# Accumulating transfers for running outputs, and weights' maxima that cross partitions through DRAM

## The chip, the core and the metric

One core of one Trainium2 chip runs the whole program. The metric is device microseconds of one execution. The core's engines work side by side and each takes its own instructions strictly in order: TensorE (PE in the rows), VectorE (DVE), ScalarE (ACT), GpSimd (POOL) and SyncE (SP), which issues the transfers. Semaphores tie them together.

## The reference

Chunked attention (batch 4, 8 heads, 768 positions of 64, chunks of 32 with 16 positions of left and 8 of right context and 8 memory rows) makes x, 3072 tokens of 512 columns. Then a mixture of eight experts with a Sinkhorn routing P follows, and it is nearly all of the work:

```python
for e in range(E):                      # 8 experts
    h = np.maximum(x @ w1[e], 0.0)      # 3072 x 512 @ 512 x 1024
    ye = h @ w2[e]                      # 3072 x 1024 @ 1024 x 512
    out += P[:, e:e + 1] * ye
```

## The kernel before

**Units.** The expert part runs 48 units: for each of 8 experts 6 groups of 512 tokens, in alternate direction from expert to expert, so that the last group of one expert is the first of the next. A unit has 36.4 to 36.7 us in the kernel's own timetable (`begin`). It makes the hidden layer in four parts fp (`hidden`: banks px, py, pz; reads q and r on ScalarE, sums c on VectorE) and then the outputs of two token tiles at a time (`output`: banks yx, yy, yz; reads y on ScalarE). Every matrix is split into two 16-bit halves (three passes), and products of 2x2 blocks are formed with seven instead of eight multiplications, which is why there are sums of weights (ws, wsi), of hidden blocks (ss) and of products (c, acc). `inner` does the same once more inside one product (banks ix, iy, iz, tile m).

**Running outputs.** For each tile T of 128 tokens a row block `akeep[T]` of 128x512 f32 lies in DRAM. `fetch_acc` loads it into an `acc` tile (ring of four), 12 us ahead of the unit's outputs. `collect` lets GpSimd add the read product q into acc (line 2382) and VectorE then add the bank times the routing factor f (line 2392); the fourth sum of an output is VectorE's alone (line 2426). SP stores acc to `akeep[T]` or, for the last expert, to the output (line 2464). Expert 0 stores without a factor; expert 1 applies it in a ScalarE pass behind the load.

**Weights.** `maxima(e + 1)` is called in the first unit of expert e, is due three units later, and loads the next expert's 4 MB once to find the largest magnitude of each matrix. `scales` turns the per-partition maxima into scales: from expert 1 on GpSimd does `partition_all_reduce` across the partitions, VectorE the rest. Later `load` fetches the weights again, `cut` forms their sums ws on GpSimd (line 747, one ws tile in the ring), and `split` makes the two halves: ScalarE writes the first (line 639), VectorE the second (line 648). `both` adds the sums wsi for the inner products.

**Order.** All instructions are collected as tasks with an engine, a cost in us, a priority and dependencies. `Plan.run` is a list scheduler at build time: it takes at each step the task that can start first, by priority among those that could, and so writes the order of each engine's instructions. `Plan.due` sets priorities back from the time at which TensorE wants a result. Tasks with `port` share an interface of VectorE and GpSimd; the planner lets such a task start only when the other engine's is over, up to 0.3 us. From the unit LATE = 4 on (`turn`, where `plan.fill` is None) attention is over and its memory is given to more buffers. All transfers are issued by SP, in its order.

Of the kernel before, what the change touches and what calls it, by code (L numbers as in the profile page):

```python
# [12 lines left out]
F32 = mybir.dt.float32  # L13
I32 = mybir.dt.int32
AF = mybir.ActivationFunctionType
ALU = mybir.AluOpType
# [24 lines left out]
LAG = 0.04  # L41
FREE = 0.3
SUMS = 0.0
ROUTE = 50
BESIDE = (2,), (3,)
HOLD = 2.0


class Task:
# [61 lines left out]
class Plan:  # L111
# [84 lines left out]
    def due(self):  # L196

        when = {}
        for t in reversed(self.tasks[self.late :]):
            if t.eng == "PE":  # L200
                when[id(t)] = t.prio
                continue
            by = [when[id(s)] for s in t.then if id(s) in when]
            if not by:
                continue
            lag = LANDS + READY + 1.0 if t.dma else LAG + 0.15
            when[id(t)] = min(by) - lag - t.cost
            if t.frees is not None:
                when[id(t)] = min(when[id(t)], t.prio + 200.0 + HOLD)
            if t.eng in ("ACT", "DVE", "POOL"):  # L210
                t.prio = when[id(t)]

    def run(self):
# [10 lines left out]
        while left:  # L224
# [51 lines left out]
            t.start = at  # L276
            if t.size:
                self.count(t.size, at, t.cost)
            if t.port:
                at = max(at, self.held["POOL" if t.eng == "DVE" else "DVE"] - FREE)  # L280
                self.held[t.eng] = at + t.cost
            if t.dma:
                t.start = at = max(at, self.pipe - BEHIND)
# [22 lines left out]
            for s in t.then:  # L306
                s.left -= 1
                late = lag
                if s.eng == t.eng and not t.dma:
                    late = 0.0 if t.eng == "PE" or self.fill is None else LAG  # L310
                elif t.dma and self.fill is not None:

                    late = MARGIN if s.prio - t.end > FAR else RISK if t.end > 10.0 else 0.0
                s.ready = max(s.ready, t.end + late)
                if s.left == 0:
                    for e in s.engines():
                        heappush(waiting[e], (s.ready, s.n, s))
# [4 lines left out]
def tile_chunked_attn_sinkhorn_moe(  # L322
# [135 lines left out]
    def ring(name, slots):  # L458
        rings[name] = Ring(slots)
# [22 lines left out]
    ring("w2", range(4))  # L482
    ring("sm", range(2))
    ring("xi", range(2))
    ring("wi", range(2))

    def buf(kind, pool, shape, dtype, name, slot=None):
# [41 lines left out]
    def scales(part, s, u, name, deps, prio, pool=None, shift=SHIFT):  # L529
# [24 lines left out]
        soon = prio if pool is None else prio - FIRM  # L554
        t = add("DVE", 0.16, most, deps, soon)
        if pool is None:

            def everywhere():
                power(a)
                inverse(a)  # L560

            t = add(
                "POOL",
                14.0,
                lambda: nc.gpsimd.partition_all_reduce(a, m, P, bass_isa.ReduceOp.max),
                [t],
                prio,
                port=False,
            )
            return add("DVE", 1.7, everywhere, [t], prio, port=True)  # L570
# [1716 lines left out]
    def fetch_acc(n, t):  # L2287

        e, u = units[n]
        res = []  # L2290
        for T in (u * TU + t, u * TU + t + TH):
            a = buf("acc", apool, [P, DM], F32, f"acc_{e}_{T}")
            ld = None
            if e > 0:
                ld = add(
                    "SP",
                    1,
                    lambda a=a, T=T: nc.sync.dma_start(a.t, akeep[T]),
                    [akept[T]],
                    outputs_at(n) - 12.0,  # L2300
                    [a],
                    dma=0.95,
                )
            if e == 1:
                ld = add(
                    "ACT",
                    0.73,
                    lambda a=a, T=T: nc.scalar.activation(
                        a.t, a.t, AF.Copy, scale=pscale[:, 0, T : T + 1]
                    ),  # L2310
                    [ld, pscales[0]],
                    outputs_at(n) - 3.0,
                    [a],
                )
            res.append((T, a, ld))
        return res

    def output(n, t, hs):
# [44 lines left out]
            )  # L2363

        lo, hi = slice(0, DH), slice(DH, DM)

        def collect(acc, ld, cols, src, q, deps, f, last=True):

            if e == 0:
# [2 lines left out]
                    0.43,  # L2372
                    lambda: nc.vector.tensor_tensor(acc.t[:, cols], src.t, q.t, op=ALU.add),
                    deps,
                    now[0] - FIRM,
                    [acc, q],
                    frees=src if last else None,
# [41 lines left out]
        c12 = collect(a2, l2, hi, pz, q6, [t3, r6], f2)  # L2419
        yield  # L2420
        t4 = run(px, P4, True, [c22])
        if e > 0:
            c21 = add(
                "DVE",
                0.49,
# [18 lines left out]
        for T, a, deps in ((T2, a2, [c11, c12]), (T1, a1, [c22, c21])):  # L2444
            dst = out[T * P : (T + 1) * P] if e == E - 1 else akeep[T]
            if n == len(units) - 1:

                for cols, dep in zip((lo, hi) if a is a2 else (hi, lo), deps):
# [8 lines left out]
                        [a],  # L2457
                        dma=0.7,
                    )
                continue  # L2460
            akept[T] = add(
                "SP",
# [219 lines left out]
    for n, (e, u) in enumerate(units):  # L2682
# [27 lines left out]
        if n == LATE:  # L2710
# [3 lines left out]
            def turn():  # L2714
                plan.fill = None
                astack.close()
                late["xi"] = ctx.enter_context(tc.tile_pool(name="xr", bufs=1, side="right"))
                late["wi"] = ctx.enter_context(tc.tile_pool(name="wri", bufs=1, side="right"))
                late["w2"] = ctx.enter_context(tc.tile_pool(name="wr2", bufs=1, side="right"))
# [8 lines left out]
            att_tasks = lgs + [xkept[v] for v in range(KEEP)] + list(gkept.values())  # L2728
            opened[0] = add("-", 0.0, turn, att_tasks, -2000.0)
            for kind, slot in (  # L2730
                ("xi", 0), ("xi", 1), ("wi", 0), ("wi", 1), ("w2", 4), ("w2", 5), ("h", 4), ("h", 5), ("c", 2), ("ss", 2)
            ):
                rings[kind].after(slot, [opened[0]])
            for kind in ("c", "ss"):
# [124 lines left out]
```

## Time and profile before

| | |
|---|---|
| time before, three runs | 1918.87 us median (1915.16 to 1921.62) |
| the profiled execution | 1916.56 us, span of its instructions 1914.8 us |
| TensorE's granted clock | 1.000 |
| busy, share of the span | TensorE 98%, VectorE 77%, ScalarE 54%, GpSimd 44% |
| DMA | 262.61 MB, mean 137 GB/s, 215305 packets |
| queues used by transfers | hardware queue 42.8% of the engines' time, instruction fetch under 1% |

A row names the engine, the line, the operation and its tiles as out<-in. A time in brackets is the idle time just before the row, with the instruction that ended it. Matmuls are pipelined and overlap in the rows: one of 256 columns shows 273 ns, while a group of 12 moves on by 1.31 us.

### The profile page before, as it was taken

The page shows a single profiled execution, that of the slowest core. Times are in us where ns is not written, and L with a number is a line of the kernel's source. Part 1 is how long each engine was busy: PE and PEld are TensorE (multiplying, and loading weights), DVE is VectorE, ACT ScalarE, POOL GpSimd, SP SyncE. Part 2 cuts the span into 40 slices and gives each one's busy share as a digit, 9 for nine tenths or more (in the row PEclk, how much of TensorE's full clock was granted, in tenths as well). Part 3 has the DMA queues.
Part 4 walks back from the last instruction along what each step waited for, and adds up shares of the span by engine and source line. Part 5 has one row for each costly group of instructions (what it writes and reads, how often), then busy time and mean ns, then how long its engine had stood idle before and what let it go on. Part 6 is the DMA issues. An engine that isn't in the chain of part 4 may idle for free. (4 is left out here: it accounts for less than half of the span.)

```text
span 1914.8 us, 48313 instructions
## 1 busy us (share of the span) xinstructions
PE 1881.3 (98%) x19931; PEld 1618.2 (85%) x19931; DVE 1476.4 (77%) x2446; ACT 1036.5 (54%) x2077; POOL 843.6 (44%) x851
## 2 busy tenths in 40 slices
PE   8899999999999999999999999999999999999999
PEld 5677667688889989888988989888998889889998
DVE  6887789878789776888579866897668885796565
ACT  6655555654665455555456444654555554564452
POOL 3531222643346444635454453655346354554233
PEclk9999999999999999999999999999999999999999
DMA  9968844244424541363234443245413732322422
GB/s 216 214 138 205 213 143 144 95 143 179 153 67 148 207 148 45 116 231 140 94 107 153 155 141 103 73 167 193 142 46 115 248 123 99 107 95 89 138 84 67
DMA packets 215305, 262.61 MB, mean 137 GB/s; under 512 B 111148, under 2 KB 144940, under 8 KB 210732
## 3 DMA queue, kind: packets, MB, share of 16 engines
q1 hardware_dynamic: 215084, 259.52, 42.8%
q8 instruction: 156, 2.56, 0.6%
q14 instruction: 65, 0.53, 0.1%
HBM read 194.46 MB, written 65.01 MB: 136 GB/s over the span
## 5 line engine op out<-in xcount | busy, mean ns | idle before, releaser
L1900 PEld LDWEIGHTS <-w 128*128 128x128 f16 x7188 | 700.3, 98 | 91.9 <-issue 8.9
L1900 PEld LDWEIGHTS <-h 128*128 128x128 f16 x7056 | 682.7, 98 | 81.9 <-issue 4.6
L1900 PE MATMUL px<-x,w 128*128 128x256 f16 x4512 | 544.6, 273 | 5.8 <-ACT q L2060 4.8
L1900 PE MATMUL yx<-w,h 128*128 128x256 f16 x4032 | 468.5, 273 | 4.3 <-DVE acc L2392 3.8
L2382 POOL TENSOR_TENSOR acc<-acc,y 128x256 f32<-128x256 f32 x252 | 247.0, 995 | 286.0 <-ACT y L2357 227.9
L1900 PE MATMUL pz<-x,w 128*128 128x256 f16 x2256 | 278.1, 273 | 0.0
L1900 PE MATMUL yz<-w,h 128*128 128x256 f16 x2016 | 233.8, 273 | 0.0
L2126 POOL TENSOR_TENSOR c<-h,m 128x256 f32<-128x256 f32 x118 | 99.8, 854 | 286.0 <-ACT h L2110 181.9
L2250 ACT CAST h<-ss 128x1024 f16<-128x1024 f32 x168 | 174.9, 1041 | 62.9 <-DVE ss L2208 62.2
L2258 DVE SCALAR_TENSOR_TENSOR h<-c,h 128x768 f16<-128x768 f32 x168 | 197.4, 1177 | 14.1 <-ACT h L2220 12.0
L2208 DVE SCALAR_TENSOR_TENSOR ss<-c,ss 128x256 f32<-128x256 f32 x336 | 197.8, 589 | 5.9
L2276 POOL TENSOR_TENSOR h<-ss,h 128x1024 f16<-128x1024 f32 x68 | 157.7, 2320 | 96.4 <-ACT h L2250 82.2
L2220 ACT ACTIVATE h<-c 128x768 f16<-128x768 f32 x168 | 140.8, 839 | 100.9 <-DVE c L2070 98.8
L1976 ACT ACTIVATE m<-ix 128x256 f32<-128x256 f32 (+1 forms) x105 | 36.4, 346 | 227.8 <-PE ix L1949 224.0
L2070 DVE SCALAR_TENSOR_TENSOR c<-pz,q 128x256 f32<-128x256 f32 x188 | 77.9, 420 | 97.0 <-PE pz L1900 87.6
L2208 DVE SCALAR_TENSOR_TENSOR ss<-c,h 128x256 f32<-128x256 f32 (+1 forms) x252 | 149.1, 592 | 3.1 <-POOL h L2276 2.0
L2276 DVE TENSOR_TENSOR h<-ss,h 128x1024 f16<-128x1024 f32 x100 | 139.0, 1390 | 0.9 <-ACT h L2250 0.8
L2579 PE MATMUL yp<-w,h 128*128 128x512 f16 x576 | 131.7, 379 | 0.0
L2060 ACT ACTIVATE q<-px 128x256 f32<-128x256 f32 x258 | 96.1, 383 | 61.1 <-PE px L1900 60.2
L1900 PE MATMUL yy<-w,h 128*128 128x256 f16 x1008 | 116.9, 273 | 0.0
L2357 ACT ACTIVATE y<-yx,pscale 128x256 f32<-128x256 f32 x168 | 78.6, 471 | 57.6 <-PE yx L1900 55.6
L2392 DVE SCALAR_TENSOR_TENSOR acc<-yx,pscale,acc 128x256 f32<-128x256 f32 x84 | 40.2, 479 | 89.9 <-POOL acc L2382 71.2
(197 smaller groups left out, 2302.2 us busy)
## 6 DMA issues: line engine op xcount, KB each, us to landing
x<-xkeep SPq DMA_DIRECT2D x28, 1792.0 KB
akeep<-acc SPq DMA_DIRECT2D x168, 256.0 KB
acc<-akeep SPq DMA_DIRECT2D x168, 256.0 KB
w1f<-in_moe_w_dram SPq DMA_DIRECT2D x36, 512.0 KB
w2f<-in_moe_w_dram SPq DMA_DIRECT2D x32, 512.0 KB
w1fm<-in_moe_w_dram SPq DMA_DIRECT2D x28, 512.0 KB
w2fm<-in_moe_w_dram SPq DMA_DIRECT2D x28, 512.0 KB
xkeep<-x SPq DMA_DIRECT2D x6, 1792.0 KB
```

What stands on the lines that cost most here:

```text
L1900: nc.tensor.matmul(dst.t, a, b, start=(not more and n == 0), stop=(n == end), skip_group_check=more,)
L2060: lambda: nc.scalar.activation(t.t, src.t, AF.Copy, scale=DOWN),
L2070: lambda: nc.vector.scalar_tensor_tensor(c.t[:, o], src.t, DOWN, q.t, op0=ALU.mult, op1=ALU.add),
L2126: lambda: nc.gpsimd.tensor_tensor(c.t[:, 2], rr(0), m[1](), op=ALU.add),
L2208: lambda: nc.vector.scalar_tensor_tensor(dst(), src(), 0.0, other(), op0=ALU.max, op1=op),
L2220: lambda: nc.scalar.activation(h.t[:, 0, 0:3], c.t, AF.Relu),
L2250: lambda: nc.scalar.copy(h.t[:, 0, 3:7], ss.t),
L2258: lambda: nc.vector.scalar_tensor_tensor(h.t[:, 1, 0:3].rearrange("p a n -> p (a n)"), c.t.rearrange("p a n -> p (a n)"), 0.0, h.t[:, 0, 0 ...
L2276: lambda: spare.tensor_tensor(h.t[:, 1, 3:7], ss.t, h.t[:, 0, 3:7], op=ALU.subtract),
L2357: (lambda: nc.scalar.activation(t.t, src.t, AF.Copy, scale=f))
L2382: lambda: nc.gpsimd.tensor_tensor(acc.t[:, cols], acc.t[:, cols], q.t, op=ALU.add),
L2579: nc.tensor.matmul(py.t, hf.t[:, hl, where[fh], o : o + P], room(fp, WIDE * wl + DM * fh, WIDE * wl + DM * (fh + 1)), start=(fp == 0 and i ...
```

## The change

1. Experts 2 to 6 (`grows`) do not load the running output. `collect` becomes one VectorE instruction, bank times f plus q, written to acc; the fourth sum becomes a ScalarE copy with the factor. GpSimd issues a transfer that adds acc to `akeep[T]` in DRAM; it waits for the earlier transfer to the same rows.
2. From unit LATE on, the weights' maxima go to DRAM (128x2 values) and come back to every partition as 128x256, both issued by SP, and VectorE reduces them. The result waits for a ring `mr` of one tile.
3. The planner, after attention, no longer keeps VectorE's and GpSimd's `port` tasks apart; it lets them overlap and lengthens both by 0.4 of the overlap. It counts 0.8 us more until another engine sees a GpSimd result, and 2.4 us (`ASKED`) for GpSimd to issue an accumulating transfer. So the whole order after attention is made anew.

```diff
+ASKED = 2.4
+SHARED = 0.4
+BESIDES = 0.8
@@ Plan.due
-            when[id(t)] = min(by) - lag - t.cost
+            late = BESIDES if t.eng == "POOL" else 0.0
+            when[id(t)] = min(by) - lag - late - t.cost * (1.0 + SHARED / 2 if t.port else 1.0)
@@ Plan.run
-            if t.port:
+            if t.port and self.fill is not None:
                 at = max(at, self.held["POOL" if t.eng == "DVE" else "DVE"] - FREE)
+                self.held[t.eng] = at + t.cost
+            elif t.port and not t.dma:
+                other = "POOL" if t.eng == "DVE" else "DVE"
+                both = min(max(self.held[other] - at, 0.0), t.cost)
+                t.cost += SHARED * both
+                clock[other] += SHARED * both
+                self.held[other] += SHARED * both
                 self.held[t.eng] = at + t.cost
...
+                elif t.eng == "POOL" and self.fill is None and not t.dma:
+                    late = BESIDES
@@ scales
+            bounced = opened[0] is not None
...
+            if bounced:
+                kept = dram.tile([P, n], F32, name=f"mkeep_{name}")
+                t = add("SP", 1, lambda: nc.sync.dma_start(kept, m), [t], prio, dma=0.3)
+                whole = rings["mr"].take(
+                    lambda k: late["mr"].tile([P, P * n], F32, tag="mr", name=f"mr_{name}")
+                )
+                t = add(
+                    "SP",
+                    1,
+                    lambda: nc.sync.dma_start(
+                        whole.t, kept.rearrange("p c -> (p c)").partition_broadcast(P)
+                    ),
+                    [t],
+                    prio,
+                    [whole],
+                    dma=0.5,
+                )
+
+                def gathered():
+                    nc.vector.tensor_reduce(
+                        a, whole.t.rearrange("p (q c) -> p c q", c=n), axis=AX.X, op=ALU.max
+                    )
+                    everywhere()
+
+                return add("DVE", 1.5, gathered, [t], prio, [whole], port=True)
@@ fetch_acc
-            if e > 0:
+            if e == 1 or e == E - 1:
@@ output
+        grows = 1 < e < E - 1
...
+            if grows:
+                return add(
+                    "DVE",
+                    0.49,
+                    lambda: nc.vector.scalar_tensor_tensor(
+                        acc.t[:, cols], src.t, f, q.t, op0=ALU.mult, op1=ALU.add
+                    ),
+                    deps + ready,
+                    now[0] - FIRM,
+                    [acc, q],
+                    frees=src if last else None,
+                )
...
-        if e > 0:
+        if grows:
+            c21 = add(
+                "ACT",
+                0.5,
+                lambda: nc.scalar.activation(a1.t[:, lo], px.t, AF.Copy, scale=f1),
+                [t4] + ready,
+                now[0] - FIRM,
+                [a1],
+                frees=px,
+            )
+        elif e > 0:
...
+            if grows:
+                akept[T] = add(
+                    "POOL",
+                    ASKED,
+                    lambda a=a, dst=dst: nc.gpsimd.dma_start(dst, a.t, accum_op=ALU.add),
+                    deps + [akept[T]],
+                    now[0],
+                    [a],
+                    dma=1.9,
+                )
+                continue
```

What this does to the order of the engines is shown at three places, in rows of the built programs. Names end in the tile's number; `L2382` is a line of the program that the row is from.

**GpSimd, third unit of expert 5** (c are sums for the hidden blocks, `ISA` are the all-reduce and the switches of GpSimd's configuration around it, `ws_6_0` the cut of the next expert's weights). Before:

```order
L2126 TENSOR_TENSOR c_4_2_19083<-h_4_2_19069,m_4_1_18850 128x256
L2126 TENSOR_TENSOR c_4_3_19096<-h_4_3_19080,m_4_1_18850 128x256
L565 ISA
L565 ISA most_of<-most_of 128x2
L2382 ISA
L2382 TENSOR_TENSOR acc_18_19085<-acc_18_19085,y_5_4_0_19295 128x256
L2382 TENSOR_TENSOR acc_19_19107<-acc_19_19107,y_5_4_1_19304 128x256
L2126 TENSOR_TENSOR c_3_0_19248<-h_3_0_19167,m_4_1_18850 128x256
```

Changed:

```order
L2166 TENSOR_TENSOR c_4_2_18927<-h_4_2_18900,m_4_1_18679 128x256
L2166 TENSOR_TENSOR c_4_3_18940<-h_4_3_18909,m_4_1_18679 128x256
L787 TENSOR_TENSOR ws_6_0_18992<-w2f_0_18865 128x256
L2166 TENSOR_TENSOR c_3_0_19004<-h_3_0_18994,m_4_1_18679 128x256
L787 TENSOR_TENSOR ws_6_0_18992<-ws_6_0_18992,w2f_0_18865 128x256
```

The all-reduce and the acc sums are gone, and the next cut follows at once.

**GpSimd, hand-over from expert 4 to 5** (`ws_5_2` and `ws_5_3` are cuts of w2's third and fourth part, `akeep` rows are accumulating transfers). Before:

```order
L747 TENSOR_TENSOR ws_5_2_18478<-w2f_2_17983,ws_5_2_18478 128x256
L747 TENSOR_TENSOR ws_5_3_18592<-w2f_3_18425 128x256
L747 TENSOR_TENSOR ws_5_3_18592<-ws_5_3_18592,w2f_3_18425 128x256
L747 TENSOR_TENSOR ws_5_3_18592<-w2f_3_18425 128x256
L747 TENSOR_TENSOR ws_5_3_18592<-w2f_3_18425,ws_5_3_18592 128x256
L2126 TENSOR_TENSOR c_4_0_18653<-h_4_0_18641,m_4_0_18301 128x256
```

Changed:

```order
L787 TENSOR_TENSOR ws_5_2_18170<-w2f_2_17781,ws_5_2_18170 128x256
L2528 DMA akeep_162<-acc_22_18145 128x512
L2528 DMA akeep_163<-acc_23_18151 128x512
L2528 DMA akeep_160<-acc_20_18250 128x512
L2528 DMA akeep_161<-acc_21_18272 128x512
L787 TENSOR_TENSOR ws_5_3_18381<-w2f_3_18191 128x256
```

Four issues stand between the two cuts.

**ScalarE at the same hand-over** (`w_5_2` is the first half of that part, q and `h<-px` are the reads that TensorE waits for). Before:

```order
L639 ACTIVATE w_5_2_18490<-w2f_2_17983,sw 128x256
L639 ACTIVATE w_5_2_18490<-ws_5_2_18478,sw 128x1024
L2060 ACTIVATE q_5_5_2_18566<-px_5_2_18492 128x256
L2060 ACTIVATE q_5_5_3_18571<-px_5_3_18501 128x256
L2060 ACTIVATE q_5_5_2_18582<-pz_5_2_18559 128x256
L639 ACTIVATE w_5_3_18520<-w2f_3_18425,sw 128x256
L2060 ACTIVATE q_5_5_3_18594<-pz_5_3_18573 128x256
L2220 ACTIVATE h_5_2_18630<-c_5_2_18535 128x768
L2110 ACTIVATE h_4_0_18641<-px_4_0_18621 128x256
L2110 ACTIVATE h_4_1_18651<-px_4_1_18632 128x256
L639 ACTIVATE w_5_3_18520<-ws_5_3_18592,sw 128x1024
```

Changed, first the split of the third part, then that of the fourth:

```order
L679 ACTIVATE w_5_2_18339<-ws_5_2_18170,sw 128x1024
L2479 ACTIVATE acc_21_18272<-yx_5_1_18055,pscale 128x256
L2016 ACTIVATE m_4_0_18147<-ix_4_0_18129 128x128
L2100 ACTIVATE q_5_5_2_18368<-px_5_2_18332 128x256
```

```order
L2100 ACTIVATE q_5_5_3_18423<-pz_5_3_18404 128x256
L679 ACTIVATE w_5_2_18339<-w2f_2_17781,sw 128x256
L679 ACTIVATE w_5_3_18402<-w2f_3_18191,sw 128x256
L679 ACTIVATE w_5_3_18402<-ws_5_3_18381,sw 128x1024
L2260 ACTIVATE h_5_2_18468<-c_5_2_18379 128x768
L2150 ACTIVATE h_4_0_18477<-px_4_0_18452 128x256
L2150 ACTIVATE h_4_1_18485<-px_4_1_18461 128x256
```

The third part's split moved ahead of all reads of px, the fourth part's from behind the reads `h_4<-px` to ahead of them.

## Rows read from the trace of the kernel before

**Rows 1.** The page, busy time, share of the span and instructions of each engine.
```profile
PE 1881.3 (98%) x19931; PEld 1618.2 (85%) x19931; DVE 1476.4 (77%) x2446; ACT 1036.5 (54%) x2077; POOL 843.6 (44%) x851
```

**Rows 2.** Stretches: PE, PEld, DVE, ACT, POOL busy, clock, DMA share, GB/s.
```profile
400.00:1880.00 1480.00, 1464.42 (x13982) 1315.55 (x13980) 1144.57 (x1862) 795.42 (x1606) 687.19 (x678) 1.00 0.38 131
```

**Rows 3.** TensorE's waits over the span: total us, times, longest us.
```profile
PE ix L1949 <- DVE m L1987: 6.3, 4, 1.6
PE px L1900 <- ACT q L2060: 4.8, 6, 1.0
PE yx L1900 <- DVE acc L2392: 3.8, 5, 1.0
```

**Rows 4.** Timeline of TensorE at place A: start us, us, what, idle before.
```profile
1552.68 1.47 PE L1900 MATMUL yx<-w,h 128*128 128x256 f16 x12 [0.80 <-DVE acc L2392]
...
1556.06 0.49 PE L1949 MATMUL ix<-xi,w 128*128 128x128 f16 x6 [1.57 <-DVE m L1987]
```

**Rows 5.** Timeline of GpSimd ahead of place A.
```profile
1520.18 1.42 POOL L2126 TENSOR_TENSOR c<-h,m 128x256 f32<-128x256 f32 x2 [6.21 <-DVE m L1987]
1530.37 0.37 POOL L565 PARTITION_ALL_REDUCE most_of<-most_of  x1 [8.77 <-DVE ss L2208]
1538.06 1.40 POOL L2382 TENSOR_TENSOR acc<-acc,y 128x256 f32<-128x256 f32 x2 [7.32 <-ACT w L639]
```

**Rows 6.** Timeline of VectorE there: the maximum, ss sums, acc, a weight split.
```profile
1521.20 0.16 DVE L540 TENSOR_REDUCE most_of<-mxs 128x2 f32<-128x8 f32 x1
...
1548.49 0.95 DVE L2208 SCALAR_TENSOR_TENSOR ss<-c,ss 128x256 f32<-128x256 f32 x1
...
1552.14 0.48 DVE L2392 SCALAR_TENSOR_TENSOR acc<-yx,pscale,acc 128x256 f32<-128x256 f32 x1 [1.98 <-POOL acc L2382]
...
1552.94 2.34 DVE L648 SCALAR_TENSOR_TENSOR w<-ws,sw,w 128x1024 f16<-128x1024 f32 x1
...
1555.60 0.41 DVE L1987 SCALAR_TENSOR_TENSOR m<-ix,m 128x256 f32<-128x256 f32 x1
```

**Rows 7.** Timeline of TensorE at place B, a hand-over.
```profile
1707.37 1.47 PE L1900 MATMUL px<-x,w 128*128 128x256 f16 x12 [0.75 <-ACT q L2060]
...
1713.92 1.47 PE L1900 MATMUL px<-x,w 128*128 128x256 f16 x12
```

**Rows 8.** Timeline of ScalarE at place B.
```profile
1705.90 1.15 ACT L639 ACTIVATE w<-ws,sw 128x1024 f16<-128x1024 f32 x1 [2.16 <-POOL ws L747]
...
1709.99 0.84 ACT L2220 ACTIVATE h<-c 128x768 f16<-128x768 f32 x1 [1.45 <-DVE c L2070]
1710.85 0.38 ACT L2110 ACTIVATE h<-px 128x256 f32<-128x256 f32 x1
1711.59 1.15 ACT L639 ACTIVATE w<-ws,sw 128x1024 f16<-128x1024 f32 x1 [0.36 <-POOL ws L747]
```

**Rows 9.** Timeline of GpSimd at place B.
```profile
1704.70 1.17 POOL L747 TENSOR_TENSOR ws<-w2f,ws 128x256 f32<-128x256 f32 x1
1708.45 0.92 POOL L747 TENSOR_TENSOR ws<-w2f 128x256 f32<-128x256 f32 x1 [2.58 <-DVE w L648]
```

**Rows 10.** A stretch ahead of place A, columns as in rows 2.
```profile
1515.00:1530.00 15.00, 15.00 (x146) 13.52 (x144) 11.42 (x22) 7.71 (x18) 1.42 (x2) 1.00 0.97 350
```

**Rows 11.** GpSimd's costliest groups: count, busy us, mean ns, idle before.
```profile
L2382 POOL TENSOR_TENSOR acc<-acc,y 128x256 f32<-128x256 f32 x252 | 247.0, 995 | 286.0 <-ACT y L2357 227.9 <-ACT w L639 45.6 <-DMA acc<-akeep 10.0
L2276 POOL TENSOR_TENSOR h<-ss,h 128x1024 f16<-128x1024 f32 x68 | 157.7, 2320 | 96.4 <-ACT h L2250 82.2 <-PE px L1900 14.0
```

**Rows 12.** SP's stores of acc: duration ns min/median/max, first and last start us.
```profile
L2464 SPq DMA_DIRECT2D akeep<-acc x144: 319/320/1731, 401.6 to 1703.3; - x144
```

**Rows 13.** Timeline of VectorE at place B.
```profile
1699.28 0.87 DVE L2392 SCALAR_TENSOR_TENSOR acc<-yz,pscale,acc 128x256 f32<-128x256 f32 x2
...
1707.09 1.28 DVE L648 SCALAR_TENSOR_TENSOR w<-ws,sw,w 128x1024 f16<-128x1024 f32 x1 [0.94 <-ACT w L639]
```

**Rows 14.** Groups of VectorE and ScalarE, columns as in rows 11.
```profile
L2426 DVE SCALAR_TENSOR_TENSOR acc<-yx,pscale,acc 128x256 f32<-128x256 f32 x84 | 39.8, 478 | 30.6 <-PE yx L1900 30.6
L2357 ACT ACTIVATE y<-yx,pscale 128x256 f32<-128x256 f32 x168 | 78.6, 471 | 57.6 <-PE yx L1900 55.6 <-POOL acc L2382 0.8
```

More of the change, by code (lines that the diff above doesn't have):

```diff
@@ L484, in tile_chunked_attn_sinkhorn_moe @@
     ring("xi", range(2))
+    ring("mr", range(1))
     ring("wi", range(2))
@@ L2716, in turn @@
                 astack.close()
+                late["mr"] = ctx.enter_context(tc.tile_pool(name="mr", bufs=1, side="right"))
                 late["xi"] = ctx.enter_context(tc.tile_pool(name="xr", bufs=1, side="right"))
@@ L2730, in tile_chunked_attn_sinkhorn_moe @@
             for kind, slot in (
-                ("xi", 0), ("xi", 1), ("wi", 0), ("wi", 1), ("w2", 4), ("w2", 5), ("h", 4), ("h", 5), ("c", 2), ("ss", 2)
+                ("mr", 0), ("xi", 0), ("xi", 1), ("wi", 0), ("wi", 1), ("w2", 4), ("w2", 5), ("h", 4), ("h", 5), ("c", 2), ("ss", 2)
             ):
```

## The prediction

> **What bounds the kernel now.** First the busy shares on the page: TensorE is busy 1881.3 us of a span of 1914.8, VectorE 77% of it [rows 1]. So the question is only which waits of TensorE the change removes or adds. The stretches come next: between 400 and 1880 us, where the changed code works, TensorE misses 1480 - 1464.42 = 15.6 us, at a granted clock of 1.00 [rows 2]. The table of TensorE's waits names them [rows 3]: ix on VectorE's m 6.3 us in 4 pieces, px on ScalarE's q 4.8 us in 6, yx on VectorE's acc 3.8 us in 5. Nothing else of TensorE can be won there.
>
> The timeline shows two places. **Place A** comes four times, three units into an expert: yx waits 0.80 us and just after it ix waits 1.57 [rows 4]. Upstream stands GpSimd [rows 5]: it ends two c sums at 1521.6, runs the all-reduce of the maxima at 1530.37, and starts its next add only at 1538.06, 16.5 us that hold nothing else. The backlog reaches VectorE, whose acc waited 1.98 us for GpSimd's add until 1552.14; the weight split behind it then takes 2.34 us beside GpSimd's work, and m, which ix waits for, stands behind both [rows 6]. These four places make all of the 6.3 and the 3.8, **10.1 us**. Six all-reduces lie in this stretch, so two cost TensorE nothing.
>
> **Place B** is the hand-over to a new expert, five times: px waits 0.75 us for q [rows 7]. ScalarE runs in order, and ahead of q stands a split of ws that starts at 1705.90, after 2.16 us of idle [rows 8], when GpSimd's cut of that weight ends at 1704.70 + 1.17 [rows 9]. Five times 0.76 is **3.8 us**; the sixth wait of that kind, the longest with 1.0 us, is at another place.
>
> **The change, part by part.** The six late all-reduces go (the seventh, of expert 1, stays). Each is replaced by two small transfers on SP's queue and a reduction over 256 columns on VectorE. GpSimd gets its 16.5 us back, and the sums, cuts and adds of the backlog can start on time: -10.1 us, between 0 (something else holds GpSimd there) and -10.1. The crossing itself I cost at nothing: VectorE's new reduction stands behind the ss sums of the next unit's first two parts, which in the trace of before ended 28 us after the maximum was known (1521.20 to 1549.4) [rows 6]. On SP's queue it goes behind two weights and a load of x (the DMA engines' share is 0.97 there [rows 10]). If it landed later than that cover, VectorE would stand still with acc sums and weight splits behind it.
>
> GpSimd loses 180 of 252 adds at 0.995 us, 179 us [rows 11], and gets 120 accumulating transfers to issue. The trace of before has no transfer issued by GpSimd. Bounds of one issue from the nearest rows: 0.32 us, what SP's sequencer needs for the same tile [rows 12], and 2.32 us, GpSimd's longest frequent row [rows 11]. I take 2.0 us, twice 0.995, the two adds that covered as many columns, because that is GpSimd's own pace and the nearer side to be wrong on: 240 us, 61 more than before on an engine busy 687 of 1480 us [rows 2]. That load is hidden; what counts is where the issues stand.
>
> They come in fours behind each unit's outputs. At the hand-over all four stand between the cuts of ws for w2's third and fourth part (the order rows). The fourth cut began at 1708.45 [rows 9], and ScalarE's split of it, at 1711.59 [rows 8], cost TensorE nothing. In the new order the reads of px stand behind this split, and TensorE needs the first at 1713.92 [rows 7], less 0.38 for the read, 0.84 for a relu and 1.15 for the split [rows 8]: the cut may end at 1711.5 and begin at 1708.4, no later than before. The first issue waits for VectorE's last sum of its tile, which ended at 1699.7 (half of the pair at 1699.28) [rows 13]. If the third cut is done by then, four issues fit up to (1708.4 - 1699.7)/4 = **2.2 us** each. At 2.0 they cost nothing; at 2.32 they cost 4 x 0.12 us at 5 hand-overs, 2.4 us; beyond 2.2, 20 us for every us of issue.
>
> Place B: the split that q stood behind moves ahead of the last reads of acc, but the fourth part's split, with its own wait on GpSimd, moves ahead of the reads of px. I take half, -1.9, with bounds 0 and -3.8.
>
> Moved from VectorE to ScalarE is one sum per output, 60 in all: 0.48 us less on one and 0.47 more on the other, a few us an expert, hidden on both [rows 14]. SP loses 120 loads and 120 stores, for which no TensorE wait stands in the table [rows 3]. In five experts acc tiles are not loaded any more, so they must be free only when the next unit's sums write them, half a unit on; four issues at 2.0 us and a landing fit. The last expert loads what the accumulates of the unit before wrote; there too half a unit lies between.
>
> An accumulating transfer reads a tile on chip and one in DRAM and writes one, where a store and a load moved two. Between no more time than these and half as much again, it adds at most 120 x 0.75 us = 90 us (256 KB at the 350 GB/s of [rows 10] is 0.75 us) to 1480 us with a share of 0.38 [rows 2]: hidden, except where x is loaded at 0.97.
>
> TensorE's own order is unchanged but for a few instructions before 400 us. The sum against the profiled execution, 1916.56 us: -10.1 - 1.9 = -12.0, 1904.6. The median of the three runs, 1918.87, is 2.3 us higher and gives 1906.9. Between the two I say **1906**. About 0.3%, 5.8 us, is what a measurement of this kernel can tell from no change, so "same" means 1913 to 1925.
>
> One rule speaks against the change. What the rows show first: VectorE's long work here is sums of two inputs, and the same split of 1024 columns takes 1.28 us at the hand-over [rows 13] and 2.34 us in place A, with GpSimd at work [rows 6]; the two engines do hold each other up. The Trainium skill (SBUF — State Buffer, on who interferes with whom) says that a transfer issued from GpSimd starves for descriptors while VectorE runs in a two-port mode, as its copies can, and gives some 620 ns for one alone and 3100 ns beside a copy. By the rule alone, two-input sums leave descriptors free and the sum stays; with its 3100 ns at every issue the sum would be 18 us higher. No row of before shows either.
>
> **The rivals.**
>
> *Slower: the issues hold GpSimd.* If VectorE's sums block them, as they stretch GpSimd's adds and are stretched by them, one may take 4.0 us. Then the fourth cut at every hand-over is 4 x 1.8 = 7.2 us late, ScalarE stands at its split with px's reads behind it, and TensorE loses 36 us over five: 1906 + 36 = 1942. It decides from 2.2 us on, and the whole is slower than the bound from 2.2 + 19/20 = 3.15 us. For it: four stand in a row where VectorE is busiest. Against it: 3.15 us is more than GpSimd's longest frequent row. Chance 0.14. The rule above would work in this way.
>
> *No difference: the gain is paid back.* Issues of 2.5 to 3 us do it: at 2.7 us, +10, 1916. So would accumulates that push a load of x behind them by 1 to 2 us in six units. For it: no row excludes either, and at place A four issues stand among the new expert's cuts too. Against it: the margin of 2.2 us was taken from a hand-over that still had place B's wait in it. Chance 0.17.
>
> *The scale comes late through DRAM,* so that place A's wait only changes its releaser: if the row lands more than 28 us after the maximum, VectorE stops. At 2 us each, six times, 12 us: 1918. Against it: the queue ahead of it is under 3 MB, 8 us at 350 GB/s. Chance 0.03.
>
> **How the numbers follow.** The forecast has 0.66, with a range of its own of 1900 (both places gone, -13.9, on the lowest run, 1915.16, gives 1901) to 1912. Faster 0.66; same 0.17 + 0.03 = 0.20; slower 0.14. The range 1900 to 1921 leaves out the slower rival and little else.
>
> **What would show it.** Right: the waits of ix on m and of yx on acc are gone, GpSimd has no gap of 16 us three units into an expert, and TensorE misses 3 to 5 us between 400 and 1880. GpSimd's issue rows give the price that I took as 2.0. Wrong: TensorE's px waits on ScalarE's reads at five hand-overs, with the fourth cut of ws behind the issues; or ix waits for x.

## The result, and the profile after

The changed kernel takes 1895.32 us (median of four runs, 1893.51 to 1896.18) beside 1917.01 us for the kernel before (four runs): a ratio of 0.9883, 95% interval 0.9861 to 0.9905, 21.7 us faster. Forecast were 1906 us and a range of 1900 to 1921. The direction was right; the time lies 4.7 us below the range, and the gain is nearly double the 12 us of the sum.

Busy time of TensorE on the page of the changed kernel:

```profile
PE 1876.8 (99%) x19931; PEld 1618.5 (86%) x19931; DVE 1426.5 (75%) x2392; ACT 1066.8 (56%) x2137; POOL 780.9 (41%) x785
```

The stretch that answers to [rows 2], with the same columns:

```profile
400.00:1880.00 1480.00, 1479.55 (x14158) 1333.00 (x14156) 1100.50 (x1819) 832.32 (x1677) 625.89 (x620) 1.00 0.41 111
```

TensorE now misses 0.45 us there, where it missed 15.6. VectorE is down by 44 us and GpSimd by 61; the forecast had GpSimd 61 us *up*. None of the three waits of [rows 3] is left; TensorE's table for this stretch has one other row:

```profile
PE px L1940 <- DVE c L2110: 0.4, 1, 0.4
```

Upstream, VectorE's waits for GpSimd's sums into acc, in the same stretch, before and then after (total us, times, longest):

```profile
DVE acc L2392 <- POOL acc L2382: 80.6, 27, 4.8
```

```profile
DVE acc L2445 <- POOL acc L2435: 6.6, 3, 4.4
```

The first row is a sign of where to look that no row ahead of the prediction gave: 27 waits of VectorE behind GpSimd's adds, 80.6 us. It does not say how much is to be won. Two of the kernels below, e1_bounce_only and then e3_planner_only, have

```profile
DVE acc L2445 <- POOL acc L2435: 67.5, 28, 4.8
```

```profile
DVE acc L2445 <- POOL acc L2435: 8.0, 12, 1.8
```

The first keeps most of these waits and wins 11 us, the second has nearly none left and wins 7.

**A measure that waits don't give.** In every unit one px group stands between a yx group and a yy group of TensorE, and its start is a landmark in both traces; from one to the next is a unit. Here are landmarks of before from TensorE's timeline: first another one, the first px group behind 400 us, then one ahead of the hand-overs, the two ends of a unit at place A, the two ends of one at place B, and the last.

```profile
404.77 1.47 PE L1900 MATMUL px<-x,w 128*128 128x256 f16 x12
...
717.27 1.47 PE L1900 MATMUL px<-x,w 128*128 128x256 f16 x12
...
1534.33 1.47 PE L1900 MATMUL px<-x,w 128*128 128x256 f16 x12
...
1573.42 1.47 PE L1900 MATMUL px<-x,w 128*128 128x256 f16 x12
...
1683.02 1.47 PE L1900 MATMUL px<-x,w 128*128 128x256 f16 x12
...
1720.47 1.47 PE L1900 MATMUL px<-x,w 128*128 128x256 f16 x12
...
1829.69 1.47 PE L1900 MATMUL px<-x,w 128*128 128x256 f16 x12
```

And the same seven of the changed kernel:

```profile
400.33 1.47 PE L1940 MATMUL px<-x,w 128*128 128x256 f16 x12
...
712.55 1.47 PE L1940 MATMUL px<-x,w 128*128 128x256 f16 x12
...
1514.56 1.47 PE L1940 MATMUL px<-x,w 128*128 128x256 f16 x12
...
1550.97 1.47 PE L1940 MATMUL px<-x,w 128*128 128x256 f16 x12
...
1660.32 1.47 PE L1940 MATMUL px<-x,w 128*128 128x256 f16 x12
...
1696.86 1.47 PE L1940 MATMUL px<-x,w 128*128 128x256 f16 x12
...
1806.08 1.47 PE L1940 MATMUL px<-x,w 128*128 128x256 f16 x12
```

Between the second and the last lie thirty units: 1829.69 - 717.27 = 1112.42 us before, 1806.08 - 712.55 = 1093.53 now, **18.9 us** less. The unit at place A fell from 39.09 to 36.41 us, the hand-over from 37.45 to 36.54. A further 4.44 us lie ahead of the first landmark (404.77 and 400.33). Together with 0.3 between the first two landmarks and -0.2 behind the last this is the 23.4 us by which the spans differ.

The first sign of a right forecast held: the waits of ix on m and of yx on acc are gone, and TensorE misses even less than the 3 to 5 us named. The price of an issue, 120 times (duration ns min, median, max):

```profile
L2528 POOL DMA_DIRECT2D akeep<-acc x120: 828/865/1703, 618.8 to 1680.2; - x120
```

And at a hand-over, where four issues stand between two cuts (first and last issue, first and last row of the fourth cut):

```profile
1675.08 0.88 POOL L2528 DMA_DIRECT2D akeep<-acc  x1 [4.62 <-DVE acc L2424]
...
1680.19 0.86 POOL L2528 DMA_DIRECT2D akeep<-acc  x1 [1.48 <-ACT m L2016]
1681.26 0.73 POOL L787 TENSOR_TENSOR ws<-w2f 128x256 f32<-128x256 f32 x1 [0.20 <-DVE w L688]
...
1683.76 1.17 POOL L787 TENSOR_TENSOR ws<-w2f,ws 128x256 f32<-128x256 f32 x1
```

The issues wait for their tiles, not for GpSimd; the cut follows 0.2 us behind the last.

### The profile page after: what moved, and what is told of

The parts are those of the page before. It is cut to its first block, busy times and chain, and to the rows that moved or that the text cites. A ratio compares the mean times of both kernels' runs of the same rounds, so it can differ in the third digit from the quotient of the medians.

```text
span 1891.4 us, 47796 instructions
## 1 busy us (share of the span) xinstructions
PE 1876.8 (99%) x19931; PEld 1618.5 (86%) x19931; DVE 1426.5 (75%) x2392; ACT 1066.8 (56%) x2137; POOL 780.9 (41%) x785
## 4 chain that ended last, share of the span: by engine, by line
PE 95%; DVE 2%; DMA 1%; POOL 1%; ACT 0%; issue 0%; SPq 0%; POOLq 0%; DVEq 0%
PE px L1940 26%; PE yx L1940 23%; PE pz L1940 13%; PE yz L1940 12%; PE yy L1940 6%; PE yp L2653 5%; PE py L1940 2%; PE ix L1989 2%; PE iz L1989 1%; PE sp L1317 1%; PE xp L1395 1%; PE pp L2570 1%; PE iy L1989 1%; PE tk L1250 0%; PE ta L1384 0%; DVE mxs L725 0%
## 5 line engine op out<-in xcount | busy, mean ns | idle before, releaser
L2298 DVE SCALAR_TENSOR_TENSOR h<-c,h 128x768 f16<-128x768 f32 x168 | 182.8, 1089 | 12.9 <-ACT h L2260 11.0
L2528 POOL DMA_DIRECT2D akeep<-acc x120 | 104.9, 933 | 108.3 <-DVE acc L2424 76.3
L2316 DVE TENSOR_TENSOR h<-ss,h 128x1024 f16<-128x1024 f32 x100 | 126.5, 1272 | 1.9 <-ACT h L2290 1.8
L2435 POOL TENSOR_TENSOR acc<-acc,y 128x256 f32<-128x256 f32 x72 | 71.6, 1005 | 103.4 <-ACT y L2397 77.5
L787 POOL TENSOR_TENSOR ws<-w1f 128x256 f32<-128x256 f32 x64 | 62.5, 977 | 114.1 <-DVE w L688 56.9
```

The lines of the kernel that those rows point to most:

```text
L2298: lambda: nc.vector.scalar_tensor_tensor(h.t[:, 1, 0:3].rearrange("p a n -> p (a n)"), c.t.rearrange("p a n -> p (a n)"), 0.0, h.t[:, 0, 0 ...
L2316: lambda: spare.tensor_tensor(h.t[:, 1, 3:7], ss.t, h.t[:, 0, 3:7], op=ALU.subtract),
L2528: lambda a=a, dst=dst: nc.gpsimd.dma_start(dst, a.t, accum_op=ALU.add),
```

## The experiments

The change has three parts that can be had apart: the accumulating transfers (T), the crossing through DRAM (D), the planner's new rules (R). Six kernels give the missing combinations. Of each profile the landmarks give the time of the same thirty units, and what it exceeds the changed kernel's by at place A (four units and the four ahead of them) and at the hand-overs B (five, and the five ahead). With none of the three parts the program is the kernel before, instruction for instruction. Each ratio is to runs of the kernel before taken beside it, whose medians lie between 1915.5 and 1918.1 us.

| kernel | parts | median us | ratio to before, 95% | thirty units us | A | B |
|---|---|---|---|---|---|---|
| before, two profiles | none | 1917.01 | 1 | 1112.4, 1111.3 | 12.4, 12.1 | 6.5, 5.7 |
| e1_bounce_only | D | 1906.69 | 0.9946 (0.9932 to 0.9960) | 1101.3 | 2.0 | 5.8 |
| e2_grow_only | T | 1901.11 | 0.9917 (0.9902 to 0.9932) | 1099.6 | 6.1 | 0.0 |
| e3_planner_only | R | 1908.64 | 0.9952 (0.9938 to 0.9966) | 1105.5 | 4.0 | 6.2 |
| e4_no_planner | T, D | 1906.56 | 0.9941 (0.9926 to 0.9956) | 1101.8 | 8.3 | 0.0 |
| e5_no_bounce | T, R | 1895.85 | 0.9894 (0.9880 to 0.9907) | 1093.5 | 0.0 | 0.0 |
| e6_no_grow | D, R | 1908.53 | 0.9962 (0.9948 to 0.9975) | 1103.2 | 3.5 | 6.2 |
| changed, two profiles | T, D, R | 1895.32, 1897.27 | 0.9883, 0.9905 (0.9890 to 0.9921) | 1093.5, 1093.6 | 0.0 | 0.0 |

**e1_bounce_only**, from the changed kernel: no accumulating transfers, old rules.

```diff
-SHARED = 0.4
-BESIDES = 0.8
+SHARED = 0.0
+BESIDES = 0.12
...
-            late = BESIDES if t.eng == "POOL" else 0.0
+            late = 0.0
...
-            if t.port and self.fill is not None:
+            if t.port:
...
-            if e == 1 or e == E - 1:
+            if e > 0:
...
-        grows = 1 < e < E - 1
+        grows = False
```

> The kernel before with one part of the change alone: the late maxima cross partitions through DRAM; loads, GpSimd's adds and the old planner's rules stay. Theory 1 (the 16.5 us in which the all-reduce keeps GpSimd are the whole of place A): the four long units of place A fall from 39.1 to 39.7 us to 36.4 us, 11.6 us in all, the five hand-overs stay at 37.5 us, time 11 to 12 us under the kernel before. Rival (GpSimd's 252 adds are the cause and the all-reduce only sets the place): the four units stay above 38 us, gain under 5 us. Of the first 400 us, where the order of every engine is the one of before: if the 4.4 us that the changed kernel is ahead there come from its order, the first unit's landmark stays at 404.8 us within 1 us; if they are scatter of the transfers at the start, it moves freely between 400 and 405.

Theory 1 held. Three of the four units of place A come down to 36.4 us (one keeps 1.0), the hand-overs keep theirs, the wait of [rows 7] again:

```profile
1696.90 1.36 PE L1940 MATMUL px<-x,w 128*128 128x256 f16 x11 [0.75 <-ACT q L2100]
```

So with GpSimd's adds in place, the all-reduce's outage is what makes place A.

**e2_grow_only**: the rules undone as above (the first three places of that diff), and the all-reduces kept.

```diff
-            bounced = opened[0] is not None
+            bounced = False
```

> The kernel before with the accumulating transfers alone; the all-reduces and the old planner's rules stay. Theory 1 (the 16.5 us of the all-reduce are place A): the four units stay above 38 us, at most 5 us are won. Rival (the adds behind the all-reduce are the backlog, and without them 16.5 us of GpSimd cost nothing): the four units fall to 36.4 us, 11 to 12 us are won. Hand-overs: if the wait there comes from the order of ScalarE, they stay at 37.5 us unless the order moves.

The rival held too, and the gain is larger than its 11 to 12 us: all four units of place A are at 36.40 us although the all-reduces are there, and the hand-overs are cured as well, at 36.54, by the transfers alone. At a hand-over the third cut of ws now ends early:

```profile
1688.74 0.73 POOL L787 TENSOR_TENSOR ws<-w2f,ws 128x256 f32<-128x256 f32 x1
```

That is 1689.47, 1.0 us behind the unit's first px at 1688.46; before it ended at 1705.87 [rows 9], 4.7 us behind the px at 1701.22. What this kernel loses, 6.1 us, is a new wait in the four units ahead of place A. VectorE's order puts a maximum of the next weights ahead of two c sums, and that waits for its load; TensorE stands behind them (one of the four, VectorE's rows, then TensorE's):

```profile
1294.03 1.22 DVE L725 TENSOR_REDUCE mxs<-w2fm 128x1 f32<-128x1024 f32 x1 [2.18 <-DMA w2fm<-in_moe_w_dram]
1295.17 0.74 DVE L2110 SCALAR_TENSOR_TENSOR c<-px,q 128x256 f32<-128x256 f32 x2
```

```profile
1295.63 1.47 PE L1940 MATMUL px<-x,w 128*128 128x256 f16 x12 [1.70 <-DVE c L2110]
```

**e3_planner_only**: the changed kernel without transfers (as in e1) and without the crossing (as in e2).

> The kernel before with the planner's new rules alone (overlap of VectorE and GpSimd at 0.4, 0.8 us more for GpSimd's results). Theory (the hand-overs are a matter of order): the five fall from 37.5 to 36.5 us, 5.2 us; place A stays, since the all-reduce is still there. With the 4.4 us of the first 400 us if they are a matter of order: 9 to 10 us under the kernel before; 5 us if they are scatter. Rival (order does nothing without the transfers): no difference.

Half right. The rules cure the hand-overs, but the unit ahead of each grows by 1.0 us, so that B stays at 6.2; and they lower place A, to 4.0, which I had not expected of them (1.7 us more lie in the units behind it). The wait that takes B's place (the table of TensorE's waits behind 600 us, then one of them):

```profile
PE yx L1940 <- DVE acc L2445: 5.4, 5, 1.1
```

```profile
1655.38 2.78 PE L1940 MATMUL yx<-w,h 128*128 128x256 f16 x24 [1.09 <-DVE acc L2445]
```

Ahead of that acc sum VectorE has two runs of weight splits:

```profile
1645.44 4.09 DVE L688 SCALAR_TENSOR_TENSOR w<-w1f,sw,w 128x512 f16<-128x512 f32 x4
1649.45 3.14 DVE L688 SCALAR_TENSOR_TENSOR w<-ws,sw,w 128x1024 f16<-128x1024 f32 x1
...
1654.86 0.47 DVE L2445 SCALAR_TENSOR_TENSOR acc<-yx,pscale,acc 128x256 f32<-128x256 f32 x1
```

In the changed kernel the same two read

```profile
1630.92 2.19 DVE L688 SCALAR_TENSOR_TENSOR w<-w1f,sw,w 128x512 f16<-128x512 f32 x4
...
1633.66 3.13 DVE L688 SCALAR_TENSOR_TENSOR w<-ws,sw,w 128x1024 f16<-128x1024 f32 x1
```

The split of 1024 columns takes as long there; the four of 512 columns are 1.9 us shorter. In this kernel GpSimd has cuts and adds into acc beside them. That those 1.9 us are what delays the acc sum is likely and was not tried by itself. With the adds in, the new order moves a wait of about the same size, it does not remove it. The 4.4 us of the first 400 us are not there: the first landmark stands at 404.04.

**e4_no_planner**: only the rules undone (the first three places of e1's diff).

> The changed kernel with the old planner's rules: transfers and crossing through DRAM stay. Theory (the three parts add up: place A by the crossing, hand-overs and the first 400 us by the order): 9 to 10 us above the changed kernel, 1904 to 1906, with hand-overs of 37.5 us. Rival (the new transfers empty GpSimd so far that order does not matter): within 3 us of the changed kernel.

Both missed. At 1906.56 us the time is 0.6 us above the theory's range, and not for its reason: the hand-overs are at 36.54 us, and the 8.3 us lie in the units ahead of and at place A, where px waits for c as in e2 (4.4 us in 4) and ix for loads of x (3.0 us in 2). I did not follow these row by row.

**e5_no_bounce**: only the all-reduces kept (the diff of e2).

> The changed kernel with the all-reduces kept: accumulating transfers and the planner's new rules. Theory after the first four runs (either the adds gone or the all-reduce gone frees place A, and the new rules place what is left): 36.4 us in all units of expert 2 to 6 but for up to 1 us at the four places where the all-reduce stands, 1895 to 1899. Rival (the planner can't place a 16.5 us outage that it counts as 14): four units of 37.4 to 38.6 us as in the run with the transfers alone, 1900 to 1903.

The theory held, and this settles what the crossing is worth in the changed kernel: nothing that can be measured. Between the landmarks it is 1093.5 us like the changed kernel, and yet GpSimd's outage is all there (GpSimd's timeline):

```profile
1282.26 1.44 POOL L2166 TENSOR_TENSOR c<-h,m 128x256 f32<-128x256 f32 x2 [0.16 <-ACT h L2150]
1291.78 0.37 POOL L605 PARTITION_ALL_REDUCE most_of<-most_of  x1 [8.09 <-DVE ss L2248]
1301.21 1.41 POOL L2166 TENSOR_TENSOR c<-h,m 128x256 f32<-128x256 f32 x2 [9.06 <-issue]
```

From 1283.70 to 1301.21 GpSimd does nothing but the all-reduce, 17.5 us, 1 us longer than at [rows 5]; TensorE misses no more than in the changed kernel:

```profile
400.00:1880.00 1480.00, 1479.57 (x14159) 1333.16 (x14158) 1083.19 (x1816) 829.39 (x1676) 622.65 (x626) 1.00 0.41 111
```

**e6_no_grow**: only the transfers undone (the last two places of e1's diff).

> The changed kernel with loads, stores and GpSimd's adds kept: the crossing through DRAM and the planner's new rules. Theory (GpSimd's adds between ScalarE's read and VectorE's sum are what the new rules, with 0.8 us more for each GpSimd result, can't place ahead of the hand-over): the unit before each hand-over stays at 37.8 us as with the rules alone (5 x 1.0 us), place A gone, 1900 to 1904. Rival (freed of the all-reduce, the new rules reach the changed kernel without transfers): 1894 to 1897.

The theory held for the hand-overs (37.8 us in the units ahead of them) and missed at place A, which keeps 3.5 us, and in the time: 1908.53 us, 13 us above the changed kernel. The rules and the crossing without the transfers gain no more than the crossing alone.

**e10_adds_back**: the all-reduces kept (as in e2), and 180 adds on GpSimd that no one waits for. The line that makes the tile `spare` is left out here.

```diff
+                add(
+                    "POOL",
+                    0.74,
+                    lambda: nc.gpsimd.tensor_tensor(spare[0], q.t, q.t, op=ALU.add),
+                    deps[1:],
+                    now[0] - FIRM,
+                    [q],
+                )
```

> The changed kernel with the all-reduces kept (1895.85 us above) and with 180 adds on GpSimd put back that nobody waits for: each adds ScalarE's read to itself into a spare tile at the place where the sum into acc stood. It has more sums than the reference needs, its output is not changed by them. Theory (place A was VectorE standing behind GpSimd's sums): GpSimd is as busy as before and nobody waits for it, within 3 us of 1896. Rival (place A was GpSimd's load itself, the cuts and c sums behind the adds coming late): four units of 38 us and more, 1903 to 1910.

It takes 1896.52 us, ratio 0.9899 (0.9885 to 0.9913). GpSimd is busier than in the kernel before (768 us to 687), has the outage as well (17.6 us, from 1284.49 to 1302.13), and TensorE misses 0.44 us:

```profile
400.00:1880.00 1480.00, 1479.56 (x14157) 1332.87 (x14155) 1125.53 (x1817) 831.82 (x1675) 767.91 (x806) 1.00 0.41 111
```

VectorE's rows are stretched by it again, 1125.53 us in this stretch where e5 has 1083.19, and that reaches TensorE nowhere. So it is not GpSimd's load that made the waits. What the transfers take away besides is the 180 places at which VectorE's order stood behind a GpSimd add, the loads of acc, and 19 us of VectorE's own work (1144.57 us in this stretch of before). That the dependence is what counts fits VectorE's waits for the adds; no run parts it from the other two.

**e7_four_pieces**: the price of an issue raised, the order kept.

```diff
-                    lambda a=a, dst=dst: nc.gpsimd.dma_start(dst, a.t, accum_op=ALU.add),
+                    lambda a=a, dst=dst: [
+                        nc.gpsimd.dma_start(
+                            dst[:, c : c + DM // 4], a.t[:, c : c + DM // 4], accum_op=ALU.add
+                        )
+                        for c in range(0, DM, DM // 4)
+                    ],
```

> The changed kernel, its order unchanged, each accumulating transfer issued in four pieces of 128 columns: if a piece costs what a whole one does (0.87 us), a tile's issue costs 3.5 us and the four tiles of a unit hold GpSimd 14 us. The prediction's rule (room of 2.2 us for each of the four issues at a hand-over, 20 us for every us beyond): 20 x 1.3 = 26 us above the changed kernel, with TensorE's px waiting on ScalarE's reads behind the fourth cut. Rival (issues of smaller pieces cost in proportion, 0.22 us): no difference within 3 us. Second rival (the next unit has slack, so that only part of the lateness reaches TensorE): 5 to 15 us above.

2001.76 us, ratio 1.0448 (1.0430 to 1.0467): 106 us above the changed kernel, with the expected wait, and four times the price of the rule. A hand-over, GpSimd's rows, then the split of ws on ScalarE and TensorE's px:

```profile
1777.49 1.76 POOL L2529 DMA_DIRECT2D akeep<-acc  x2
1781.64 12.44 POOL L2529 DMA_DIRECT2D akeep<-acc  x14 [2.38 <-DVE acc L2424]
1790.63 4.20 POOL L787 TENSOR_TENSOR ws<-w2f 128x256 f32<-128x256 f32 x1
...
1796.27 0.72 POOL L787 TENSOR_TENSOR ws<-w2f,ws 128x256 f32<-128x256 f32 x1
```

```profile
1797.03 1.15 ACT L679 ACTIVATE w<-ws,sw 128x1024 f16<-128x1024 f32 x1 [6.63 <-POOL ws L787]
```

```profile
1799.22 2.72 PE L1940 MATMUL px<-x,w 128*128 128x256 f16 x12 [3.55 <-ACT h L2150]
```

The px group takes 2.72 us in place of 1.47, because the granted clock fell behind the stall, from 2.4 to 1.2 GHz (columns as in [rows 2]):

```profile
1799.30:1802.60 3.30, 3.30 (x17) 2.32 (x17) 3.27 (x6) 2.63 (x8) 0.77 (x1) 0.50 0.94 378
1802.70:1880.00 77.30, 77.30 (x751) 69.76 (x750) 50.09 (x90) 37.58 (x77) 27.12 (x26) 1.00 0.32 115
```

From the first issue behind the tile's end (1781.64) to the end of the cut's first row (1794.83) are 13.2 us for 14 pieces and a row of 0.9: 0.88 us a piece, as much as a whole transfer. The durations of such a burst overlap and its last part is booked on the cut, so only the ends count. Of the 95.3 us that the thirty units lose, the hand-overs and the units ahead of them have 36.3 (I had 26), place A with the units ahead has 43.8, and nine of the other twelve units lose 1.6 us or a little more, which the rule did not see. The granted clock has a part in this too: nine stretches of 3.4 to 10.2 us among the thirty units are at 0.50, and TensorE is busy for 32 us of them. At full clock half of that would do, so an estimate is 16 of the 95.3 us, about 7 of them at the hand-overs. No other kernel here has such a stretch among the thirty units.

**e9_two_pieces**: the same with `DM // 2`.

> The changed kernel, its order unchanged, each accumulating transfer in two pieces of 256 columns. The run in four pieces showed 0.87 us for a piece of any size, so a tile's issue costs 1.74 us, near the 2.0 us of the prediction. The prediction's rule (nothing is lost up to 2.2 us): within 2 us of the changed kernel. Rival (from the run in four pieces: 107 us for 2.6 us more an issue, shared by all units): 0.87/2.6 of it, 36 us above. Between them: a loss at the hand-overs and place A only, 10 to 15 us.

1897.64 us, ratio 0.9902 (0.9886 to 0.9918), beside 1897.27 for the changed kernel measured with it; thirty units in 1093.7 us. The room that the prediction worked out, 2.2 us an issue, is not contradicted: 1.74 us costs 0.2 us at place A and nothing else, and the 3.5 us of e7 cost much. Nothing between the two was tried.

**e8_asked**: the planner's cost of an issue.

```diff
-ASKED = 2.4
+ASKED = 0.94
```

> The changed kernel with the planner's cost of an issue at 0.43 us in place of 1.10 us (it multiplies by 0.46; the issue took 0.87 us in the trace). Theory (the new order has room): within 2 us of the changed kernel. Rival (orders this close are a lottery): 3 to 10 us above, with new waits of TensorE on VectorE's c or ScalarE's q. Of the first 400 us: a fourth run of that order; the first unit's landmark at 400 us if it is a matter of order, between 400 and 405 if it is scatter.

1897.32 us, ratio 0.9905 (0.9891 to 0.9919), thirty units in 1093.6: the same. The order has room for either price. (Ahead of the prediction I gave 2.4 us as the price that the planner counts. It multiplies by 0.46, so it counted 1.10 us, near the 0.87 measured; I had missed that line.)

**e11_before_again** and **e12_after_again**: no edit.

> The kernel before once more, for the first 400 us alone: if the changed kernel's 4.4 us there are scatter of the transfers at the start, the first unit's landmark comes between 400 and 405 us; if they are a matter of order, at 404 to 405.

> The changed kernel once more. Scatter: the first unit's landmark between 400 and 405 us; order: at 400 to 401. Units as in its first profile, 1405.7 us from the first to the last landmark.

First landmarks of before: 404.77 and 401.90. Of the changed kernel: 400.33 and 404.21. Two profiles of one program lie 2.9 and 3.9 us apart, so most of the 4.4 us ahead of 400 us can be scatter of the start, where TensorE waits for loads of q and k among others; the twelve new profiles have this landmark between 401.9 and 406.0, in no order of the parts. The change itself is worth what the thirty units show, 18.9 us, or 17.7 against the second profile of before; the second measurement gives 1897.27 beside 1915.52, 18.3.

## Why the prediction was wrong in its size

The forecast named the two places rightly and the way the time would go; two terms of its sum were too small, and place B far more so than place A. The sum had 12.0 us, the thirty units show 18.9.

- **"Nothing else of TensorE can be won there", 15.6 us.** This failed first. The stretch held 18.9 us. A listed wait is shorter than the time lost: at place B px starts at 1707.37 with an idle time of 0.75 [rows 7], but the group ahead of it, at 1705.15, is 1.31 us long at full pace, so 1707.37 - 1706.46 = 0.91 is lost. The end of a group is booked 0.16 us late (a duration of 1.47 for a pace of 1.31), and a stall of about that size is in no table of waits: the units ahead of the hand-overs were 0.24 us too long and have no row there, only a px group of 1.72 us at 1667.05. The row ahead of 1707.37 reads

```profile
1705.15 1.47 PE L1900 MATMUL pz<-x,w 128*128 128x256 f16 x12
```

- **Place A, -10.1.** Measured -12.4, 2.3 more: nine waits at 0.16 make 1.4 by the same booking, and two of the four units ahead were 0.4 us too long. Its place was right. The reason was half right: I gave the whole to the all-reduce's removal and costed the removal of the adds as load, at nothing. By e1 and e2 either of the two takes away the long units (one of the four keeps 1.0 us in e1); by e5 and e10 the crossing is worth nothing once VectorE no longer waits for the adds. The rows were there [rows 6]: acc waited 1.98 us for GpSimd's add, and I read past it, upstream to the outage.
- **Place B, -1.9, "I take half".** This is the term that failed most. Measured -6.5, the units ahead included (-5.7 against the second profile of before): 4.6 more, two thirds of the miss, and outside its own bounds of 0 and -3.8. The half was no row, only a split between those bounds. Without the acc sums between them, GpSimd's cuts come 3.6 us earlier against TensorE (e2); neither the fourth cut nor ScalarE's split ahead of the reads of px delays anything.
- **2.0 us for an issue.** Measured 0.87, from 0.83 to 1.70. It lay inside the bounds of 0.32 and 2.32, and cost the forecast nothing, since below 2.2 us the sum had no term; it kept much of 0.31 of the chance on rivals that needed more than 2.2 us.
- **The Trainium skill's rule** (SBUF — State Buffer, on who interferes with whom: descriptors starve while VectorE copies in a two-port mode): the page's 3100 ns are the time of a whole transfer, which the prediction set for GpSimd's issue. No issue comes near it. With two-input sums leaving descriptors free, as the prediction read the rule, the trace agrees: 1.70 us for the longest of 120. No run here set a copy against an issue.
- **The slower rival's price.** Its mechanism is real: e7 has px behind ScalarE behind the fourth cut. At 3.5 us an issue it costs 106 us, where the rule of 20 us for each us beyond 2.2 gave 26. For the hand-overs alone that was not far off: 36.3 us, of which about 7 are the lower clock. But place A and the plain units pay as well.
- **The crossing costs nothing, the added DMA traffic is hidden, the moved sum is hidden, half a unit lies between accumulate and load.** All held: TensorE has no wait for a transfer in the stretch.
- **The range.** 1900 was the lowest run less the waits of both places, 13.9. The thirty units alone, 1918.87 - 18.9, give 1900.0; with the median of before in the comparison, 1917.01, they give 1898.1. The last 2.8 us to 1895.32 are no more than the start's scatter (3 to 4 us between two profiles of one program), which the prediction left out; its three runs were spread over 6.5 us.

## What to carry to other kernels

Look in the trace for the engine that stands *between* the bound and the slow one: VectorE's 80.6 us behind GpSimd's adds pointed at what the transfers cure, where TensorE's own table showed only what leaked through. How much it is worth such a sum does not tell. Where a stall has two causes in a row, as place A has (an outage, and VectorE's sums that wait behind it), removing either can cure it, and the second removal is then worth nothing: build the halves before crediting one. And take the gain of a stretch from landmarks over the pace, not from the sum of listed waits.

## What the runs showed of the hardware

An accumulating transfer issued by GpSimd costs it 0.87 us at each of the three sizes tried: 128x512, 128x256 (e9) and 128x128 (e7) all cost that, and pieces only multiply it. The software queue's row, the changed kernel and then four pieces (packets, MB, share):

```profile
q0 software_dynamic: 17280, 31.46, 11.3%
```

```profile
q0 software_dynamic: 69120, 31.49, 17.2%
```

Four times the packets for the same bytes take half as large a share again of the DMA engines' time, in a span that is 6% longer. An all-reduce across partitions, with the switches of GpSimd's configuration around it, leaves GpSimd without other rows for 13.3 to 17.8 us (seven in the kernel before), although its own row shows 0.37 to 0.52. And a stall can cost more than its own length: in e7 the granted clock was 0.50 for 3.4 us behind a stall of 3.55 us.
